# Re-fitted clock weights and a shared transfer queue in the list scheduler of a delta-rule attention and two-MoE kernel

## The chip, the cores and the metric

The kernel runs on one core of a Trainium2 chip. The metric is the device time of one execution in microseconds (us), here the median of three runs. The engines are TensorE (PE in the profile; PEld its weight loads), VectorE (DVE), ScalarE (ACT), GpSimd (POOL) and SyncE (SP), which only issues DMA transfers.

## What is computed

Three layers follow each other; the second takes the output of the first as its tokens, the third that of the second.

```python
# 1. delta rule, 4 x 8 heads, 768 positions, head size 48
k_n = k / (norm(k) + 1e-6)
for t in range(768):
    y[:, :, t] = q[:, :, t] @ state
    v_old = k_n[:, :, t] @ state
    state = state + beta[:, :, t] * outer(k_n[:, :, t], v[:, :, t] - v_old)
# 2. gated feed-forward, 3072 tokens x 384, inner size 2048
h = x @ w_in
g = h * sigmoid(h)
x = g @ w_out
# 3. eight experts, inner size 1024, every token through each of them
P = exp(x @ w_gate - max); eight rounds: rows to sum 1, columns to sum 1, P *= N / E
out = sum over e of P[:, e] * (relu(x @ w1[e]) @ w2[e])
```

## The kernel before, in words

The delta rule is worked in twelve steps of 64 positions (names end in the step: z2, c11_0; the last digit is the half of the heads). In each step the Gram products of the keys and queries (gk, gkq, gq, lines 360 to 475) give triangular systems; their inverse is worked out for two steps at a time on DVE in operations on the tiles nu and tu (line 520 on), goes to DRAM (rd, td) and comes back as rt and td11 (line 589). PE then merges it (z and r, line 609), reads the state (c, line 640), updates (d, line 657), gives the output (y) and the state's change (s, line 674) and transposes the output into tokens (t, line 707). DVE adds s to the state xs.

Two steps fill a block of 512 tokens of the second layer. For each of its 16 slices, PE makes h (x @ w_in, nine matmuls of 512 columns, line 740), ACT, DVE and POOL gate it (sg, g), and PE adds g @ w_out into x2p (line 782). Each fp32 operand is split in two parts for three products. During the first block DVE and ACT split the weights too, in seven DVE pieces per slice pair (wr, wt, lines 894 to 905). When a block is done, its logits l follow (line 831). There are six blocks; the fourth to sixth overlap the later steps. The third layer begins at about 743 us: 64 blocks of 15 products p (line 1213) and their outputs o (line 1300), with sums and residuals on DVE and POOL (line 1022) and the eight normalisation rounds beside the first of them.

No order is written out by hand. Every operation is handed to `class Order` with an engine, a cost in us, its predecessors and a priority (`op = sc.add`). `emit` walks a modelled time: at each turn it takes, of the operations that are ready first on an engine, the one of highest priority, and at the end writes all of them out by modelled start. On the chip each engine executes its own list in that order. The modelled time has four parts that matter here: `ready` adds a latency for a predecessor on another engine (LAT) and none for one on the same; `pe` models the granted clock of TensorE by slices of time, in which every PE operation leaves its weight `cols`, and a slice runs at full speed if the one before it gathered FULL; SP's transfers share one queue, in which each starts when the one before has landed; ACT's few transfers are not in that queue but have a fixed latency of 2.2 or 2.3 us. `narrow` marks the groups of small matmuls, which the model charges for a change of tiling. Before the first product of the second layer `emit` fills waits of PE with dummy matmuls (`idle`).

Of the kernel before, what the change touches and what calls it, by code (L numbers as in the profile page):

```python
# [26 lines left out]
NF = DFF // 128  # L27
# [29 lines left out]
class Order:  # L57


    QUEUES = ("SP",)  # L60
    LAT = {"PE": 0.2, "ACT": 0.16, "DVE": 0.14, "POOL": 0.1, "SP": 0.08}
# [7 lines left out]
    TICK, PHASE, FULL = 10.24 / 3, 2.63, 2000  # L69

    def add(self, engine, cost, fn, deps=(), prio=1.5, take=(), turn=None, cols=768, port=False):

        d = [x if isinstance(x, tuple) else (x, None) for x in deps]
        self.ops.append((engine, cost, fn, d, prio, take, turn, cols, port))
        return len(self.ops) - 1
# [57 lines left out]

    def emit(self, idle=None):
        self.cols, busy = {}, False
# [7 lines left out]
        while any(left.values()):  # L143
# [36 lines left out]
            else:  # L180
                if e == "PE":
                    busy = busy or cols == 4608
                    now[e] = max(now[e], IDLE)
                    while idle and not busy and t > IDLE and now[e] + 0.5 < t:
                        order.append((now[e], len(order), None))
                        now[e] = self.pe(now[e], 0.107, 256)
                    t = max(t, now[e])
                    narrow = turn == 1 and cols != 150
# [18 lines left out]
def kernel(  # L207
# [127 lines left out]
    def load_part(s, bp, part, prio):  # L335
# [4 lines left out]
        if s and not part:  # L340

            return [(op("ACT", 0.45, adma(t(a, 0), kq[s, bp, 0, :, 0]), prio=prio), 2.3),
                    (op("ACT", 0.45, adma(t(b, 0), kq[s, bp, 1, :, 0]), prio=prio), 2.3)]
# [21 lines left out]
    def gram_k(s, bp):  # L365
# [20 lines left out]
        m = op("PE", 1.07, pe, O["ke", s, bp] + ([(O["gm", s], 0.0)] if bp else []), prio=30, take=["a"] + ([] if bp else ["g"]), turn=1, cols=1088)  # L386
# [9 lines left out]
    def gram_kq(s, bp):  # L396
# [20 lines left out]
        q = op("PE", 1.07, lambda: pe(1), ld, prio=prio, take=["a"], turn=1, cols=1088)  # L417
        m = [op("PE", 1.07, lambda: pe(0), ld + [(q, 0.0)], prio=prio, take=["a"], turn=1, cols=1088), q]
# [10 lines left out]
    def units(j):  # L429
# [3 lines left out]
        for s in (2 * j, 2 * j + 1):  # L433
            for q in range(4):
# [6 lines left out]
                O["nl", j].append(op(by, 0.45 if by == "ACT" else 0.58, go, O["nd", s] + free, prio=20 if j == 0 else 3))  # L441
# [8 lines left out]
    def gram_q(s, bp):  # L450
# [13 lines left out]
        m = op("PE", 1.07, pe, O["ld", s][bp] + [O["td2", 0]], prio=5, take=["a"], turn=1, cols=1088)  # L464
# [55 lines left out]
    def tri(j, prio):  # L520
# [13 lines left out]
        if j < 2:  # L534
            roots.append(root_act(lambda: (dg, du[:, 0]), 32, [(x, 2.2 if sc.ops[x][0] == "ACT" else None) for x in O["nl", j]]
# [53 lines left out]
    def rt_load(s):  # L589
        j, o = s // 2, 64 * (s % 2)  # L590
        res = []
        for q in (1, 3, 0, 2):
# [5 lines left out]
                O["rd", j][s % 2:s % 2 + 1] + ([O["u1", s - 1, 0], O["u1", s - 1, 1]] if s else O["rt0"]), prio=12.5 + FIRST[s]))  # L598
# [7 lines left out]
        res = [(x, 2.2) if sc.ops[x][0] == "ACT" else x for x in res]  # L606
        return res, gl, t

    def merge(s):
# [19 lines left out]
        a = O["z1", s] = op("PE", 1.13, z, O["rtl", s][:2] + O["gll", s], prio=10 + FIRST[s], take=["a", "sg"], turn=1 if s else None, cols=512)  # L629
# [3 lines left out]
        c = O["r1", s] = op("PE", 1.13, r, [e1, e2] + O["tdl", s], prio=7.5 + FIRST[s], take=["a"], turn=1 if s else None, cols=512)  # L633
# [6 lines left out]
    def state_read(s, bp):  # L640
# [11 lines left out]
        a = op("PE", 1.06, pe, [O["sa", s - 1, bp]], prio=5 + FIRST[s], take=["a", "wy"], turn=1)  # L652
# [4 lines left out]
    def update(s, bp):  # L657
        x = xs[bp]

        def pe():  # L660
            w = T["w", s, bp] if s else T["kv", s][:, bp, 1]
            ps = T["d", s, bp] = psA.tile([128, H, D], F32, tag="a", name=f"d{s}_{bp}")
            for h in range(H):
                for o in (0, 64):
                    nc.tensor.matmul(out=ps[o:o + 64, h], lhsT=rt[o:o + 64, bp, h], rhs=w[o:o + 64, h], start=True, stop=True)  # L665
        a = O["u1", s, bp] = op("PE", 1.06, pe, O["rm", s] + O["rtl", s] + [O["w", s, bp] if s else O["vr", s, bp], O["xs0", bp]]
                                + ([O["h", s // 2 - 2, NF - 1]] if s >= 4 else []), prio=2 + FIRST[s], take=["a"], turn=1 if s else None)
# [783 lines left out]
```

## Time and profile before

| | |
|---|---|
| runs | 2255.64, 2266.98, 2263.58 us; median 2263.58 |
| the profiled execution | 2263.14 us, span 2261.4 us |
| mean granted clock of TensorE in it | 0.974 |
| instructions | 40411 |
| busy | PE 97%, DVE 78%, POOL 68%, ACT 45% of the span |

The span runs from the first to the last instruction; the time has 1.7 us around it. A granted clock of 1.0 is the upper of TensorE's two levels, 0.5 the lower. Times in the rows below count from the start of the span.

### The profile page before, as it was taken

The page shows a single profiled execution, that of the slowest core. Times are in us where ns is not written, and L with a number is a line of the kernel's source. Part 1 is how long each engine was busy: PE and PEld are TensorE (multiplying, and loading weights), DVE is VectorE, ACT ScalarE, POOL GpSimd, SP SyncE. Part 2 cuts the span into 40 slices and gives each one's busy share as a digit, 9 for nine tenths or more (in the row PEclk, how much of TensorE's full clock was granted, in tenths as well). Part 3 has the DMA queues.
Part 4 walks back from the last instruction along what each step waited for, and adds up shares of the span by engine and source line. Part 5 has one row for each costly group of instructions (what it writes and reads, how often), then busy time and mean ns, then how long its engine had stood idle before and what let it go on. Part 6 is the DMA issues. An engine that isn't in the chain of part 4 may idle for free.

```text
span 2261.4 us, 40411 instructions
## 1 busy us (share of the span) xinstructions
PE 2184.4 (97%) x15750; PEld 1928.4 (85%) x15750; DVE 1760.9 (78%) x2999; ACT 1023.8 (45%) x1766; POOL 1547.7 (68%) x1387
## 2 busy tenths in 40 slices
PE   8988799999999899999999999989999999999999
PEld 8877578788877778889998999979999999999998
DVE  7695857464725698888888888897888888888887
ACT  2443333334344445454444545455454444445453
POOL 0223344445337688888788888877888888888884
PEclk9887999998989899999999999999999999999999
DMA  9767132314140201101111111111101111111101
GB/s 266 186 201 167 56 72 66 81 52 95 40 108 11 84 29 31 40 29 36 35 36 36 33 38 29 43 47 39 42 29 36 36 36 36 36 36 30 42 29 50
DMA packets 127424, 136.79 MB, mean 60 GB/s; under 512 B 83392, under 2 KB 91328, under 8 KB 127232
## 3 DMA queue, kind: packets, MB, share of 16 engines
q1 hardware_dynamic: 124864, 133.55, 21.4%
q8 instruction: 124, 2.03, 0.4%
q10 hardware_dynamic: 2368, 0.66, 0.2%
q14 instruction: 68, 0.56, 0.1%
HBM read 108.47 MB, written 25.69 MB: 59 GB/s over the span
## 4 chain that ended last, share of the span: by engine, by line
PE 64%; POOL 13%; DVE 10%; DMA 5%; issue 4%; ACT 2%; SPq 1%; DVEq 0%; POOLq 0%; ACTq 0%
PE o L1300 25%; PE p L1213 20%; PE x2p L782 6%; PE h L740 5%; DVE s L1022 4%; POOL room L1022 3%; POOL wa L1022 3%; POOL wraw L1022 2%; POOL h L1022 2%; DMA ke<-in_kq 2%; PE d L665 1%; POOL wb L1022 1%; DMA nd<-ke 1%; DVE acc L1316 1%; PE y L680 1%
## 5 line engine op out<-in xcount | busy, mean ns | idle before, releaser
L1213 PE MATMUL p<-room,wa 128*128 128x512 f32 x2880 | 732.8, 395 | 2.6 <-DVE s L1022 2.6
L1213 PEld LDWEIGHTS p<-room,wa 128*128 128x128 f32 x2880 | 537.2, 189 | 95.6 <-issue 3.0
L1300 PE MATMUL o<-wb,room 128*128 128x384 f32 x2784 | 601.2, 337 | 10.6 <-POOL room L1022 3.0
L1022 DVE TENSOR_TENSOR s<-s,p 128x512 f32<-128x512 f32 x704 | 475.8, 683 | 167.8 <-ACT s L1227 85.1
L1300 PEld LDWEIGHTS o<-wb,room 128*128 128x128 f32 x2784 | 496.7, 188 | 34.8 <-DVE acc L1316 9.3
L1022 POOL TENSOR_TENSOR room<-s,room 128x512 fp32r<-128x512 f32 x232 | 321.0, 1384 | 222.0 <-ACT s L1246 117.0
L1316 DVE SCALAR_TENSOR_TENSOR acc<-o,pr,acc 128x384 f32<-128x384 f32 x708 | 415.7, 610 | 15.0 <-PE o L1300 12.6
L1300 PE MATMUL o<-wb,h 128*128 128x384 f32 x1824 | 416.5, 336 | 6.1 <-DVE acc L1316 3.7
L1300 PEld LDWEIGHTS o<-wb,h 128*128 128x128 f32 x1824 | 327.7, 188 | 27.7 <-DVE acc L1316 2.8
L1022 POOL TENSOR_TENSOR wa<-wraw,wa 128x640 fp32r<-128x640 f32 x189 | 322.4, 1718 | 2.5 <-ACT wa L1116 2.5
L1244 ACT ACTIVATE room<-s 128x512 fp32r<-128x512 f32 x232 | 145.7, 628 | 382.5 <-DVE s L1022 382.3
L1022 POOL TENSOR_TENSOR wraw<-wraw 128x256 f32<-128x256 f32 x378 | 275.0, 748 | 20.5 <-issue 10.7
L758 POOL TENSOR_TENSOR g<-sg,g 128x512 fp32r<-128x512 f32 x96 | 129.8, 1353 | 219.9 <-ACT g L754 206.0
L1246 ACT ACTIVATE s<-s 128x512 f32<-128x512 f32 x384 | 243.1, 633 | 12.2
L782 PE MATMUL x2p<-g,w 128*128 128x512 f32 x864 | 228.9, 412 | 15.5 <-DVE w L905 5.8
L1116 ACT ACTIVATE wa<-wraw 128x640 fp32r<-128x640 f32 x189 | 138.2, 731 | 224.4 <-POOL wraw L1022 213.6
L1022 DVE TENSOR_TENSOR s<-p,s 128x512 f32<-128x512 f32 x320 | 219.5, 686 | 16.7 <-PE p L1213 2.0
L740 PE MATMUL h<-x,w 128*128 128x512 f32 x864 | 216.9, 398 | 5.9 <-DVE w L905 4.1
L782 PEld LDWEIGHTS x2p<-g,w 128*128 128x128 f32 x864 | 165.1, 196 | 59.3 <-POOL g L758 10.7
L1022 POOL TENSOR_TENSOR h<-s,h 128x512 fp32r<-128x512 f32 x152 | 208.7, 1373 | 7.9 <-ACT s L1246 7.8
L1022 DVE TENSOR_TENSOR s<-s,s 128x512 f32<-128x512 f32 x192 | 207.3, 1080 | 2.5
L740 PEld LDWEIGHTS h<-x,w 128*128 128x128 f32 x864 | 161.6, 190 | 44.2 <-DVE w L905 5.9
(177 smaller groups left out, 2260.9 us busy)
## 6 DMA issues: line engine op xcount, KB each, us to landing
wraw<-in_w SPq DMA_DIRECT2D x126, 384.0 KB, 3.0
kv<-in_kv SPq DMA_DIRECT2D x12, 768.0 KB, 5.8
ke<-in_kq SPq DMA_DIRECT2D x40, 192.0 KB, 4.4
kqp<-in_kq SPq DMA_DIRECT2D x40, 192.0 KB, 4.0
nd<-ke SPq DMA_DIRECT2D x20, 256.0 KB, 4.1
gd<-ke SPq DMA_DIRECT2D x20, 256.0 KB, 2.8
kqp<-gd SPq DMA_DIRECT2D x40, 128.0 KB, 3.8
wr<-in_w_in SPq DMA_DIRECT2D x6, 768.0 KB, 5.8
```

Of the source, the lines that this page charges most:

```text
L665: nc.tensor.matmul(out=ps[o:o + 64, h], lhsT=rt[o:o + 64, bp, h], rhs=w[o:o + 64, h], start=True, stop=True)
L680: nc.tensor.matmul(out=ps[0:64, h], lhsT=t(slice(0, 112), 1)[:, h], rhs=x[0:112, 0, h], start=True, stop=True)
L740: nc.tensor.matmul(out=ps.rearrange("p (s t) -> p s t", s=2), lhsT=w[:, k, wl], rhs=X1[:, at, k, xl], start=n == 0, stop=n == 8)
L758: nc.gpsimd.tensor_tensor(out=g[:, 1], in0=T["sg", b, f], in1=f32(g)[:, 0], op=ALU.subtract)
L782: nc.tensor.matmul(out=T["x2p", b][j], lhsT=w[:, wl, 128 * j:128 * j + 128], rhs=g[:, gl], start=f == 0 and n == 0, stop=f == NF - 1 and n ...
L1022: e.tensor_tensor(out=out, in0=in0, in1=in1, op=o)
L1116: nc.scalar.activation(P2[key][:, :, 0], R(3 + 5 * g, 8 + 5 * g), AF.Copy)
L1213: nc.tensor.matmul(out=ps, lhsT=w[:, i, wl], rhs=x[:, xl], start=k == 0, stop=k == 2)
L1244: nc.scalar.activation(P2[key][:, 0], buf(x), AF.Relu)
L1246: op2("ACT", 0.52, lambda: nc.scalar.activation(buf(x), buf(x), AF.Relu), writes=[("s", n, x)], prio=PR_H)
L1300: nc.tensor.matmul(out=ps, lhsT=h[:, hl, 128 * i:128 * i + 128], rhs=w[:, wl], start=c == 0, stop=c == 5)
L1316: op2("DVE", 0.53, lambda A=A, pk=pk, t=t: nc.vector.scalar_tensor_tensor(out=A(), in0=P2[pk], scalar=P2["pr"][:, t, e:e + 1], in1=A(), op ...
```

## The change

The planner's model changes, and no operation does. A predecessor on the same engine now costs a small latency (OWN). A slice of time now also gets KEEP for having been fast itself (`fast`), FULL is halved and PHASE shifted, and the weights `cols` are other numbers for each kind of matmul: an h or x2p product, the reference with 4608 before and 1430 now, against a Gram product 1088 and 520, z and r 512 and 221, c 768 and 240, d 768 and 390, y 1440 and 480, s 768 and 530, t 768 and 241, logits 150 and 0, the third layer's products 1536 and 477, its outputs 2304 and 716, a dummy 256 and 80. `narrow` is told by these numbers. ACT's transfers (`lands`) now pass through the queue model of SP's. Line numbers move by 10 or so.

```diff
+    OWN = {"PE": 0.0, "DVE": 0.12, "ACT": 0.12, "POOL": 0.11, "SP": 0.08}
...
-    TICK, PHASE, FULL = 10.24 / 3, 2.63, 2000
+    TICK, PHASE, FULL, KEEP = 10.24 / 3, 2.53, 1000, 120
...
-                lat = 0.0 if own == engine and engine not in self.QUEUES else self.LAT[own]
+                lat = self.LAT["SP"] if self.ops[d][9] else (self.OWN if own == engine else self.LAT)[own]
...
-            k = int((t - self.PHASE) / self.TICK + 1 + 1e-6)
-            c = cost if self.cols.get(k - 1, 0) >= self.FULL else 1.85 * cost
+            k = max(0, int((t - self.PHASE) / self.TICK + 1 + 1e-6))
+            c = cost if self.fast(k) else 1.85 * cost
...
+    def fast(self, k):
+        if k < 1:
+            return False
+        if k not in self.full:
+            self.full[k] = self.cols.get(k - 1, 0) + self.KEEP * self.fast(k - 1) >= self.FULL
+        return self.full[k]
...
-                    narrow = turn == 1 and cols != 150
+                    narrow = cols in (520, 221, 240, 390, 480, 530)
...
+                    if self.ops[i][9]:
+                        end[i] = queue = max(t + 1.5, queue) + self.ops[i][9]
                     if self.ops[i][8]:
-                        port[e] = end[i]
+                        port[e] = now[e]
...
-            return [(op("ACT", 0.45, adma(t(a, 0), kq[s, bp, 0, :, 0]), prio=prio), 2.3),
+            return [op("ACT", 0.45, adma(t(a, 0), kq[s, bp, 0, :, 0]), prio=prio, lands=0.42),
...
-        m = op("PE", 1.07, pe, O["ke", s, bp] + ([(O["gm", s], 0.0)] if bp else []), prio=30, take=["a"] + ([] if bp else ["g"]), turn=1, cols=1088)
+        m = op("PE", 1.07, pe, O["ke", s, bp] + ([(O["gm", s], 0.0)] if bp else []), prio=30, take=["a"] + ([] if bp else ["g"]), turn=1, cols=520)
...
-                              prio=2, take=["m"], turn=0, cols=4608)
+                              prio=2, take=["m"], turn=0, cols=1430)
```

What it moves, by the order of instructions on each engine, stands here at three places.

PE, from the h product of slice seven of the first block to the merge z2 of step two. Before:

```order
L740 MATMUL h0_7_2288<-x1_106,w12_2174 128x512 x9
L405 MATMUL gkq9_1_1_2326<-ke9_1_2304 64x64
L405 MATMUL gkq9_1_0_2348<-ke9_1_2304 64x64
L405 MATMUL gkq10_0_1_2373<-ke10_0_2312 64x64
L782 MATMUL x2p0_0_1804<-g0_6_2322,w12_2174 128x512 x3
L782 MATMUL x2p0_0_1804<-g0_7_2365,w12_2174 128x512 x3
L405 MATMUL gkq10_0_0_2430<-ke10_0_2312 64x64
L614 MATMUL z2_2453<-rt_93,td11_94 32x32 x32
```

Now:

```order
L750 MATMUL h0_7_2217<-x1_106,w12_2121 128x512 x9
L415 MATMUL gkq8_1_0_2240<-ke8_1_2101 64x64
L792 MATMUL x2p0_0_1781<-g0_6_2238,w12_2121 128x512 x3
L624 MATMUL z2_2298<-rt_93,td11_94 32x32 x32
L792 MATMUL x2p0_0_1781<-g0_7_2269,w12_2121 128x512 x3
```

Each Gram row stands for a group of 16 matmuls, each x2p row for the first three of nine. The Gram products of the keys of steps nine and ten left the place and come later; z2 has one group of each kind ahead of it, where it had six groups.

DVE, around the state updates (xs) of steps two and three; wt and wr are tiles of a weight that is split. Before:

```order
L750 TENSOR_TENSOR sg0_9_2595<-h0_9_2555,sg0_9_2595 128x512
L701 TENSOR_TENSOR xs0_91<-xs0_91,s2_0_2662 48x384 x2
L701 TENSOR_TENSOR xs1_92<-xs1_92,s2_1_2811 48x384 x2
L701 TENSOR_TENSOR xs0_91<-xs0_91,s3_0_2941 48x384 x2
L894 TENSOR_SCALAR wt20_2343<-wt20_2343 128x768
L895 TENSOR_SCALAR wt20_2343<-wt20_2343 128x768
L897 SCALAR_TENSOR_TENSOR wt20_2343<-wr5_2141,wt20_2343 128x768
L750 TENSOR_TENSOR sg0_10_3141<-h0_10_3112,sg0_10_3141 128x512
```

Now:

```order
L760 TENSOR_TENSOR sg0_9_2477<-h0_9_2445,sg0_9_2477 128x512
L711 TENSOR_TENSOR xs0_91<-xs0_91,s2_0_2482 48x384 x2
L711 TENSOR_TENSOR xs1_92<-xs1_92,s2_1_2619 48x384 x2
L904 TENSOR_SCALAR wt20_2273<-wt20_2273 128x768
L905 TENSOR_SCALAR wt20_2273<-wt20_2273 128x768
L907 SCALAR_TENSOR_TENSOR wt20_2273<-wr5_2088,wt20_2273 128x768
L711 TENSOR_TENSOR xs0_91<-xs0_91,s3_0_2848 48x384 x2
L711 TENSOR_TENSOR xs1_92<-xs1_92,s3_1_2891 48x384 x2
L913 TENSOR_SCALAR wr5_2088<-wt20_2273 128x768
L760 TENSOR_TENSOR sg0_10_3031<-h0_10_3004,sg0_10_3031 128x512
```

Rows in between are left out. The first five pieces of weight 20 went from behind step three's first state update to ahead of it.

PE, from the state read c11_1 of the last step to the first h product of the last block. Before, with no 512-column product from y10_0 on:

```order
L647 MATMUL c11_1_7640<-xs1_92,kqp1_86 64x48
L831 MATMUL l8_7659<-wgr_64,x2_8_0_7458 128x16
L665 MATMUL d11_0_7674<-wq11_0_7638,rt_93 64x48 x16
L665 MATMUL d11_1_7703<-wq11_1_7672,rt_93 64x48 x16
L681 MATMUL y11_0_7726<-xs0_91,kqp0_85 64x48
L681 MATMUL y11_1_7749<-xs1_92,kqp1_86 64x48
L713 MATMUL t11_0_7768<-ident_62,y11_0_7766 128x128 x3
L831 MATMUL l9_7774<-wgr_64,x2_9_0_7691 128x16
L713 MATMUL t11_1_7789<-ident_62,y11_1_7772 128x128 x3
L740 MATMUL h5_0_7819<-x1_106,w0_227 128x512 x9
```

Now:

```order
L750 MATMUL h4_15_7551<-x1_106,w29_3383 128x512 x9
L723 MATMUL t10_1_7563<-ident_62,y10_1_7561 128x128 x3
L657 MATMUL c11_1_7613<-xs1_92,kqp1_86 64x48
L792 MATMUL x2p4_0_6900<-g4_15_7606,w31_3513 128x512 x3
L675 MATMUL d11_0_7641<-wq11_0_7611,rt_93 64x48 x16
L691 MATMUL y11_0_7690<-xs0_91,kqp0_85 64x48
L723 MATMUL t11_0_7732<-ident_62,y11_0_7730 128x128 x3
L841 MATMUL l8_7738<-wgr_64,x2_8_0_7658 128x16
L723 MATMUL t11_1_7753<-ident_62,y11_1_7736 128x128 x3
L841 MATMUL l9_7773<-wgr_64,x2_9_0_7757 128x16
L750 MATMUL h5_0_7812<-x1_106,w0_236 128x512 x9
```

The last products of block four, h4_15 and x2p from g4_13 to g4_15, moved in among the small groups of steps ten and eleven, and the logits l8 moved behind t11_0.

## Rows read from the trace of the kernel before

**Rows 1.** The page's busy times, all engines.

```profile
PE 2184.4 (97%) x15750; PEld 1928.4 (85%) x15750; DVE 1760.9 (78%) x2999; ACT 1023.8 (45%) x1766; POOL 1547.7 (68%) x1387
```

**Rows 2.** Busy time by stage; stretch, us, PE PEld DVE ACT POOL busy, clock, DMA, GB/s.

```profile
0.00:262.50 262.50, 229.08 (x3650) 199.13 (x3650) 196.54 (x471) 104.86 (x178) 65.73 (x69) 0.88 0.69 183
262.50:743.40 480.90, 462.58 (x4572) 378.70 (x4571) 262.77 (x487) 177.96 (x322) 235.16 (x223) 0.96 0.27 65
743.40:2261.40 1518.00, 1492.73 (x7532) 1350.59 (x7530) 1301.59 (x2043) 741.02 (x1266) 1246.76 (x1096) 1.00 0.12 38
```

**Rows 3.** The same view, five stretches of the first two stages.

```profile
460.22:467.01 6.79, 6.79 (x199) 6.18 (x198) 4.93 (x11) 2.34 (x5) 1.87 (x3) 1.00 0.57 153
548.56:571.42 22.86, 22.52 (x450) 21.05 (x450) 12.13 (x27) 7.23 (x17) 11.13 (x14) 0.70 0.49 141
644.47:669.32 24.85, 21.74 (x486) 20.37 (x485) 8.43 (x19) 9.88 (x22) 3.98 (x6) 0.79 0.24 65
182.50:212.50 30.00, 28.19 (x642) 25.71 (x638) 14.48 (x26) 11.22 (x22) 19.97 (x21) 0.77 0.77 172
212.50:274.00 61.50, 46.44 (x334) 34.54 (x334) 55.97 (x122) 21.02 (x38) 14.15 (x12) 0.92 0.25 73
```

**Rows 4.** Chain of waits, 640 to 680 us: start us, us, what.

```profile
652.35 1.13 issue
...
654.51 1.00 issue
...
659.30 3.58 PE d L665 x64
...
667.11 0.11 PE l L832
...
668.33 0.42 PE t L713 x3
```

**Rows 5.** Chain of waits, 150 to 225 us.

```profile
174.92 1.13 PE z L614 x64
...
181.71 2.00 PE d L665 x64
```

**Rows 6.** Timeline of PE from 667 us: start us, us, what, [idle before <-releaser].

```profile
669.32 8.38 PE L740 MATMUL h<-x,w 128*128 128x512 f32 x27 [0.58 <-ACT x L716]
```

**Rows 7.** Chain of waits, 610 to 640 us.

```profile
611.47 2.04 PE h L740 x9
...
628.68 0.14 issue
```

**Rows 8.** Timeline of POOL in one block of the second MoE.

```profile
991.09 1.30 POOL L1022 TENSOR_TENSOR room<-s,room 128x512 fp32r<-128x512 f32 x1
992.34 1.02 POOL L1022 TENSOR_TENSOR wb<-wraw,wb 128x384 fp32r<-128x384 f32 x1
```

**Rows 9.** Timeline of PE in the same block.

```profile
995.36 0.68 PE L1300 MATMUL o<-wb,h 128*128 128x384 f32 x3
```

**Rows 10.** Timeline of SP at the start.

```profile
14.63 1.92 SPq L439 DMA_DIRECT2D nu<-nd  x4
16.65 0.43 SPq L385 DMA_DIRECT2D nd<-gneg  x1
```

**Rows 11.** Timeline of DVE at the start.

```profile
24.04 0.19 DVE L479 TENSOR_SCALAR rta<-nu 128x32 f32<-128x32 f32 x1 [3.55 <-DMA nu<-nd]
```

**Rows 12.** Timeline of DVE, 180 to 222 us.

```profile
187.94 1.12 DVE L701 TENSOR_TENSOR xs<-xs,s 48x384 f32<-48x384 f32 x2 [4.78 <-PE s L697]
...
212.57 1.09 DVE L894 TENSOR_SCALAR wt<-wt 128x768 f32<-128x768 f32 x1
...
215.77 0.95 DVE L901 SCALAR_TENSOR_TENSOR wr<-wr 128x768 int32<-128x768 int32 x1
```

**Rows 13.** Timeline of PE from 155 us.

```profile
154.92 4.38 PE L740 MATMUL h<-x,w 128*128 128x512 f32 x18
```

**Rows 14.** Timeline of SP ahead of the first rt loads.

```profile
167.05 4.46 SPq L595 DMA_DIRECT2D rt<-rd  x4
```

More of the change, by code (lines that the diff above doesn't have):

```diff
@@ L67, in __init__, with add @@
         self.pools, self.slot = {k: [()] * n for k, n in pools.items()}, {}
-    TICK, PHASE, FULL = 10.24 / 3, 2.63, 2000
-    def add(self, engine, cost, fn, deps=(), prio=1.5, take=(), turn=None, cols=768, port=False):
+    TICK, PHASE, FULL, KEEP = 10.24 / 3, 2.53, 1000, 120
+    def add(self, engine, cost, fn, deps=(), prio=1.5, take=(), turn=None, cols=0, port=False, lands=None):
         d = [x if isinstance(x, tuple) else (x, None) for x in deps]
-        self.ops.append((engine, cost, fn, d, prio, take, turn, cols, port))
+        self.ops.append((engine, cost, fn, d, prio, take, turn, cols, port, lands))
         return len(self.ops) - 1
@@ L132, in pe @@
         return t
+    def fast(self, k):
[4 more added lines that the diff above has]
+        return self.full[k]
     def emit(self, idle=None):
-        self.cols, busy = {}, False
+        self.cols, self.full, busy = {}, {}, False
         left, wait, then = {}, [len(o[3]) for o in self.ops], {}
@@ L181, in emit @@
                 if e == "PE":
-                    busy = busy or cols == 4608
+                    busy = busy or cols == 1430
                     now[e] = max(now[e], IDLE)
@@ L340, in load_part @@
         if s and not part:
-            return [(op("ACT", 0.45, adma(t(a, 0), kq[s, bp, 0, :, 0]), prio=prio), 2.3),
-                    (op("ACT", 0.45, adma(t(b, 0), kq[s, bp, 1, :, 0]), prio=prio), 2.3)]
+            return [op("ACT", 0.45, adma(t(a, 0), kq[s, bp, 0, :, 0]), prio=prio, lands=0.42),
+                    op("ACT", 0.45, adma(t(b, 0), kq[s, bp, 1, :, 0]), prio=prio, lands=0.42)]
         return [op("SP", 0.42, dma(t(a, part), kq[s, bp, 0, :, part]), after, prio=prio),
@@ L440, in go @@
                         out=nu[r0:r0 + 16], in_=T["nd", s][32 * q:32 * q + 32, :, c0:c0 + 32].rearrange("r u c -> u r c"))
-                O["nl", j].append(op(by, 0.45 if by == "ACT" else 0.58, go, O["nd", s] + free, prio=20 if j == 0 else 3))
+                O["nl", j].append(op(by, 0.45 if by == "ACT" else 0.58, go, O["nd", s] + free, prio=20 if j == 0 else 3,
+                                    lands=0.58 if by == "ACT" else None))
     def mask_q(s, bp):
@@ L534, in tri @@
         if j < 2:
-            roots.append(root_act(lambda: (dg, du[:, 0]), 32, [(x, 2.2 if sc.ops[x][0] == "ACT" else None) for x in O["nl", j]]
+            roots.append(root_act(lambda: (dg, du[:, 0]), 32, list(O["nl", j])
                                   + ([O["td2", j - 1]] if j else []), 8, -1.0))
@@ L597, in rt_load @@
                 in_=T["rd", j][r0:r0 + 16].rearrange("u (c r) -> c u r", r=32)),
-                O["rd", j][s % 2:s % 2 + 1] + ([O["u1", s - 1, 0], O["u1", s - 1, 1]] if s else O["rt0"]), prio=12.5 + FIRST[s]))
+                O["rd", j][s % 2:s % 2 + 1] + ([O["u1", s - 1, 0], O["u1", s - 1, 1]] if s else O["rt0"]), prio=12.5 + FIRST[s], lands=0.58 if by == "ACT" else None))
         free = [O["z1", s - 1], O["r1", s - 1]] if s else []
@@ L632, in merge @@
         sc.free(a, "a", [e1, e2])
-        c = O["r1", s] = op("PE", 1.13, r, [e1, e2] + O["tdl", s], prio=7.5 + FIRST[s], take=["a"], turn=1 if s else None, cols=512)
+        c = O["r1", s] = op("PE", 1.13, r, [e1, e2] + O["tdl", s], prio=7.5 + FIRST[s], take=["a"], turn=1 if s else None, cols=221)
         sc.free(a, "sg", [c])
@@ L785, in moe_o @@
         a = O["o", b, f] = op("PE", 2.045, pe, O["g", b, f] + O["wout", f] + prev, prio=4.5,
-                              take=["x"] if f == 0 else [], turn=0, cols=4608)
+                              take=["x"] if f == 0 else [], turn=0, cols=1430)
         sc.free(O["g", b, f][0], "g", [a])
@@ L836, in cp @@
             nc.scalar.activation(T["l2", b], T["l", b][:, :, 1], AF.Copy)
-        m = op("PE", 1.25, logit, ev + [O["wg"]], prio=2, take=["a"], turn=1, cols=150)
+        m = op("PE", 1.25, logit, ev + [O["wg"]], prio=2, take=["a"], turn=1)
         e = op("ACT", 0.12, cp, [m] + ([O["lg", b - 1]] if b else []), prio=-3.5)
@@ L1274, in products @@
             O["p", n, r] = P2["pe"] = op2("PE", 0.694, pe(r), reads=[("x", r), ("wa", wn(n), OPERAND[r][0])], writes=[("p", n, r)],
-                               deps=first + [(P2["pe"], 0.0)], take=[k], turn=2, cols=1536, prio=PR_P)
+                               deps=first + [(P2["pe"], 0.0)], take=[k], turn=2, cols=477, prio=PR_P)
             if r in then:
@@ L1339, in go @@
                 fn(P2["sk", n])
-            return op2("PE", cost, go, reads=["pr"], writes=[("sk", n)], deps=[(lastw["pr"], 1.5)], take=["m"], prio=PR_S, cols=64)
+            return op2("PE", cost, go, reads=["pr"], writes=[("sk", n)], deps=[(lastw["pr"], 1.5)], take=["m"], prio=PR_S)
         def dve(cost, fns, n=None):
```

23 lines of the change are left out of this document (11 added, 12 removed).

## The prediction

> **What bounds the kernel now.** I read the page's busy times, then the busy time by stage, then the stretches of the first two stages in which the granted clock is low, and in those the chain of waits and the timelines of PE, DVE and SP.
>
> PE is busy for 97% of the span [rows 1]. By stage [rows 2]: the second MoE, 743.40 to 2261.40, has PE busy for 1492.73 of 1518.00 us at a granted clock of 1.00, so an order can give back 25 us there at the very most. The first two stages hold 743.4 us, and there the clock is 0.88 and 0.96. A clock of 0.5 is the lower level (1.2 GHz), 1.0 the upper (2.4 GHz); 0.88 over 262.5 us means (1 - 0.88) x 262.5 = 31 us in which PE got nothing for its time, idle stretches among them, and 0.96 over 480.9 means 19 us. That is the stock from which this change, which only sorts the same operations, can draw.
>
> The change moves the clock's weights, so the question is where the clock falls. The stretches [rows 3] show it: during steps nine (548.56 to 571.42) and ten/eleven (644.47 to 669.32) the clock is 0.70 and 0.79. In the first of them PE is busy for 22.52 of 22.86 us; the reader is to see that it falls there although PE has hardly a gap, in a run of small matmuls with no 512-column product of the first MoE among them. A shorter run of the same kind, step seven (460.22 to 467.01, 6.79 us), stays at 1.00. What the low level costs one group: an update d takes 3.58 us for both halves [rows 4] where it takes 2.00 at the upper level [rows 5]; and the first three h products after the run, 27 matmuls, take 8.38 us [rows 6] where nine take 2.04 [rows 7], so 8.38 - 6.12 = 2.26 us too much.
>
> **The change, part by part.** Nothing is removed and no operation is new; the count of idle dummy matmuls at the start changes by nine. All terms are moves.
>
> *Second MoE: 0.* PE's order is the same but for the small Sinkhorn matmuls. On POOL, in nearly each of 64 blocks one wb piece (1.02 us) goes ahead of the two relu residuals issued before it, h and room. In one block room ends at 991.09 + 1.30 = 992.39 [rows 8], and the outputs that read these two start at 995.36 [rows 9]; with the piece of 992.34 ahead it would end at 993.41, 1.95 us early still. The residual that feeds the block's later outputs keeps its place. Were the cover gone, it would cost up to 1 us a block; I take 0, with +1 us in all as the bound.
>
> *Steps ten and eleven: -6 (-3 to -9).* Now: 24.85 us [rows 3], of which (1 - 0.79) x 24.85 = 5.2 us are lost to the clock, 1.13 + 1.00 = 2.1 are waits of c11 for the state [rows 4], 0.58 is the wait of h5_0 [rows 6]; add 2.26 for the h products behind. That is 10.2 us over the work. In the new order the triangular inverse of these steps is issued about three iterations earlier (an h and a w_out product each, 4.1 us), z10 stands behind h4_11, and the w_out products of g4_13, g4_14 and g4_15 and the product h4_15 stand among the small ones, which took 2.04 us each. What runs bare is only from d11_0 to l9: two updates (2.00 [rows 5]), two outputs y (priced like half an update each, 1.0), two transposes (0.42) and two logits (668.33 - 667.11 = 1.2 each [rows 4]): 7.2 us, near the 6.79 us that kept the clock [rows 3]. If the clock holds, the 5.2 and the 2.26 come back, 7.5 of the 10.2. Against that l9 now follows l8 by one transpose and may wait a microsecond or so for its operand. I take 6. Lower end: the bare stretch runs at the clock that the long one had, which loses 7.2 x 0.21 / 0.79 = 1.9, the 2.26 stay, c11's waits stay, 0.58 stays: 7 left, gain 3. Upper end: all but 1.1 of c11's waits: 9.
>
> *Step nine: -1 (0 to -6).* One wide product, that of g3_15, moves from ahead of s8_1 to between t8_1 and s8_1. The bare stretch shrinks from 22.86 x 0.70 = 16.0 us of work to some 14.7; at the same clock the loss goes from 6.9 to 6.3. Were the product enough to hold the clock, 6 would come back.
>
> *The first stage: -5 (+4 to -13).* Two things carry it. At the start, the second nd1 put was issued at 16.65, behind four nu loads of 1.92 us in all [rows 10]; the last nu loads need it, and DVE stood still for 3.55 us until 24.04 [rows 11]. The put now stands before the nu loads: it can go 2.0 us earlier, they 0.4 later. I take -1.5 (0 to -2). Then DVE: from 182.5 to 212.5 it has 14.48 us of work in 30, while from 212.5 to 274.0 it has 55.97 in 61.5 and PE only 46.44 [rows 3], since the products wait for weights that DVE splits. The first weight of that second stretch begins at 212.57, behind the state update of step three; its first five pieces run from there to 215.77 + 0.95 = 216.72, 4.1 us with two short steps of the inverse among them [rows 12], and now stand ahead of that update, in the slack stretch, where the one wait shown is 4.78 us [rows 12]. If all of this goes into idle time, the saturated stretch ends 4.1 us sooner; I take -3.5. Bounds: the same 4.1 us stand in front of the state update and the chain of steps is late by it (+4.1); or the fuller PE also keeps the clock in 182.5 to 212.5, (1 - 0.77) x 30 = 6.9 more (-11). The other moves of this stage (Gram products pushed behind step three, key loads with them) fill or leave gaps that PE has either way; the rival D is about them.
>
> *Latencies on the same engine and ACT's transfers in the shared queue* change no wait on the chip by themselves: 0.
>
> The sum: 2263.1 (the profiled execution; the median of the three runs shown is 2263.58) - 5 - 1 - 6 - 0 = **2251 us**. The ends together: 2263.1 - 13 - 6 - 9 = 2235 and 2263.1 + 4 - 3 + 0 + 1 = 2265, rounded up to 2266.
>
> A measurement of this kernel tells some 0.5%, 11.3 us, from no change: faster is under 2252, slower over 2275.
>
> **The rule that speaks against the main term.** In steps ten and eleven the two waits of c11 stand just ahead of the stretch in which d took 3.58 [rows 4], so these rows alone would also fit a clock that falls for the gaps. Against it stands step nine, with 0.34 us of idle time and a clock of 0.70. The Trainium skill, TensorE: Matmul & The Clock Gate, section "HAM oscillation — how this bites in real kernels", puts a falling clock down to idle gaps of PE between bursts. By that rule the small products themselves would keep the clock and the change would gain little at the end, a sum of about 2257; step nine's row disagrees with it as the only cause.
>
> **The rivals.**
> - A, chance 0.15: the clock falls for the gaps. c11 still comes right behind s10_1 and DVE's addition of the state, so its waits (2.1 us) stay, and with them the slow d and h behind. Of the late term only about 0 to 1 is left: 2263.1 - 5 - 1 = **2257**. For it: the place of the waits. Against it: step nine.
> - B, chance 0.15: the first stage gives nothing. DVE executes in order, and one of its multiplies (sg of h0_3) and the moved weight pieces wait for POOL's roots or for wr loads; what the slack stretch takes in, the state update loses. 2263.1 - 1 - 6 = **2256**. For it: the longest DVE wait shown there, 4.78 us, ends with PE's s [rows 12]: it is a place behind a dependency, not free time at large. Against it: PE still waits for weights behind it.
> - C, chance 0.10: the change doesn't do what it says. The new weights describe the clock no better, the wide products that now stand at the end are missing elsewhere, and the low level moves with them: **2263**.
> - D, chance 0.10, slower: a z stands ahead of its data. Between the end of h0_7 (154.92 + 4.38 = 159.30) [rows 13] and z2 at 174.92 [rows 5] PE now does six groups; in the new order only one Gram group (about 1.1) and one product (2.05) are left there. The four rt loads that z2 reads were issued from 167.05 on, 4.46 us in all [rows 14]. If they come no sooner, PE stands 174.92 - 162.45 = 12.4 us in front of z2 with all products behind it. The same at z10, which goes ahead by two products and their h, 8.2 us; it starts now 0.14 us after its rt [rows 7]. 2263.1 + 12.4 + 8.2 - 6 - 1 = **2277**. It decides from the point at which rt lands no earlier than now; against it: between the last put of step nine's keys and rt SP now issues two pairs of key loads and two weight loads, of which one pair of keys stays, and the inverse for z10 moved further than z10 did.
>
> **How the numbers follow.** The forecast, both gains, has 0.50. Its own range is 2235 to 2260, and with about 0.8 of it under 2252 that gives 0.40 faster; A gives 0.03 of its 0.15 there, B 0.04: 0.47. The rest of these, and C, are within 0.5%: 0.43. D is the 0.10 slower. The range 2235 to 2266 holds the forecast, A, B and C; it leaves out D and the tails.
>
> **What would show it.** Right: in the new profile the stretch from y10_0 to h5_0 shows a clock over 0.9 and the first three h products of the last block take near 6.1 us; DVE's saturated stretch ends 3 to 4 us sooner; the second MoE still takes 1518 us within 1. Wrong: c11's waits stand with a slow d11 behind (A); the time from 0 to z4 is unchanged (B); the low-clock stretches are as long as before, elsewhere (C); PE idle for over 5 us in front of z2 or z10 (D). A second MoE that differs by more than 3 us would show that my 0 for POOL was wrong.

## The result: 1.2% slower, all of it in the second MoE

The changed kernel takes 2287.81 us (median of 4 runs, 2284.39 to 2293.97) against 2261.99 us of the kernel before (median of 4 runs, 2255.64 to 2266.98): a ratio of 1.0119, 95% interval 1.0083 to 1.0154. That is outside the range of the prediction, on the side that was given 0.10. The profiled execution took 2284.39 us with a span of 2282.6 us and a mean granted clock of 0.98. Of the runs of all kernels below, one of pool_more (4204.75 us) was far slower than the rest and is left out of its ratio.

The page's busy times of the changed kernel, for [rows 1]:

```profile
PE 2185.0 (96%) x15747; PEld 1906.0 (83%) x15747; DVE 1784.5 (78%) x2999; ACT 1027.5 (45%) x1766; POOL 1546.2 (68%) x1387
```

DVE is busy 23.6 us longer. PE's busy time is the same to 0.6 us, but only in the sum of two opposite changes: by the stages below it is 14.2 us less in the first two layers and 14.9 us more in the second MoE. The busy time by stage, cut where [rows 2] is cut (the first h of the second block, the first product of the second MoE), with the same columns:

```profile
0.00:256.80 256.80, 221.60 (x3646) 190.76 (x3646) 196.05 (x474) 104.93 (x177) 63.18 (x69) 0.90 0.74 191
256.80:731.30 474.50, 455.83 (x4574) 372.20 (x4571) 259.17 (x484) 178.38 (x323) 239.52 (x223) 0.97 0.27 64
731.30:2282.60 1551.30, 1507.60 (x7532) 1343.01 (x7531) 1329.25 (x2043) 744.19 (x1266) 1243.51 (x1096) 0.99 0.12 37
```

The reader is to see two opposite results in one. The second MoE begins at 731.3 where it began at 743.4, which is the 12 us that the prediction hoped for, though half of it is the luck of these two traces (the means over the traces of either order of the first two layers lie 5.9 us apart, see the part on the prediction); and it lasts 1551.3 us where it lasted 1518.0, a change that the prediction had put at 0 (at most +1). In it DVE is busy 27.7 us longer (1329.25 against 1301.59) for the same 2043 instructions. The clock is not the reason: in the second MoE it stood at its lower level for 16.2 us before and 17.1 us now. Which instructions of DVE, the costliest groups show, with the group of POOL's residuals (room) below them. Before:

```profile
L1022 DVE TENSOR_TENSOR s<-s,p 128x512 f32<-128x512 f32 x704 | 475.8, 683 | 167.8 <-ACT s L1227 85.1
...
L1022 DVE TENSOR_TENSOR s<-s,s 128x512 f32<-128x512 f32 x192 | 207.3, 1080 | 2.5
...
L1022 POOL TENSOR_TENSOR room<-s,room 128x512 fp32r<-128x512 f32 x232 | 321.0, 1384 | 222.0 <-ACT s L1246 117.0
```

Now:

```profile
L1032 DVE TENSOR_TENSOR s<-s,p 128x512 f32<-128x512 f32 x704 | 476.0, 684 | 189.0 <-ACT s L1237 152.9
...
L1032 DVE TENSOR_TENSOR s<-s,s 128x512 f32<-128x512 f32 x192 | 253.2, 1319 | 2.4
```

The additions with one operand in PSUM (s<-s,p) take the same time within a nanosecond. Those with both operands in SBUF (s<-s,s, three in each of the 64 blocks) went from 1080 to 1319 ns, 46 us in all (DVE's busy time grew by less, since the records of neighbouring instructions overlap). And PE's wait for DVE's accumulation, in the second MoE 5.9 us in 10 places before, is now, in the list of waits of that stage (us in total, times, the longest):

```profile
PE o L1310 <- DVE acc L1326: 22.1, 55, 1.2
```

Why an addition grows is in the timelines of one steady block. Before, DVE's three s<-s,s and what POOL did meanwhile:

```profile
1956.38 0.69 DVE L1022 TENSOR_TENSOR s<-s,s 128x512 f32<-128x512 f32 x1
...
1959.43 0.87 DVE L1022 TENSOR_TENSOR s<-s,s 128x512 f32<-128x512 f32 x1
...
1962.14 1.40 DVE L1022 TENSOR_TENSOR s<-s,s 128x512 f32<-128x512 f32 x1
```

```profile
1951.95 4.49 POOL L1022 TENSOR_TENSOR wraw<-wraw 128x256 f32<-128x256 f32 x6
1956.40 1.82 POOL L1022 TENSOR_TENSOR room<-s,room 128x512 fp32r<-128x512 f32 x1
1958.18 3.55 POOL L1022 TENSOR_TENSOR wa<-wraw,wa 128x640 fp32r<-128x640 f32 x2
1961.70 1.29 POOL L1022 TENSOR_TENSOR h<-s,h 128x512 fp32r<-128x512 f32 x1
```

The same place in the changed kernel:

```profile
1946.10 1.57 DVE L1032 TENSOR_TENSOR s<-s,s 128x512 f32<-128x512 f32 x1
...
1950.03 1.84 DVE L1032 TENSOR_TENSOR s<-s,s 128x512 f32<-128x512 f32 x1
...
1953.70 0.68 DVE L1032 TENSOR_TENSOR s<-s,s 128x512 f32<-128x512 f32 x1
```

```profile
1941.68 3.80 POOL L1032 TENSOR_TENSOR wraw<-wraw 128x256 f32<-128x256 f32 x5
1945.83 1.29 POOL L1032 TENSOR_TENSOR room<-s,room 128x512 fp32r<-128x512 f32 x1 [0.35 <-PE p L1223]
1947.07 1.19 POOL L1032 TENSOR_TENSOR wraw<-wraw 128x256 f32<-128x256 f32 x1
1948.23 3.09 POOL L1032 TENSOR_TENSOR wa<-wraw,wa 128x640 fp32r<-128x640 f32 x2
```

One swap on POOL is the difference between these rows: its six weight sums (wraw) ran through before, now the last of them stands behind the first residual room of the block (of the sum c1). Of an s<-s,s and one of these POOL instructions, the one that starts second waits for the first. Before, the sums kept POOL until DVE had begun: DVE's addition took 0.69, and room took 1.82 instead of 1.29. Now room begins at 1945.83, as soon as what it waits for is there, and DVE's addition, 0.27 us later, ends at 1947.67, that is 0.55 us after room's end at 1947.12. The second one ends at 1951.87, 0.55 us after the two wa pieces (1948.23 + 3.09 = 1951.32). The third one before (1962.14 + 1.40 = 1963.54) ends 0.55 after h (1961.70 + 1.29 = 1962.99). The Trainium skill, SBUF — State Buffer, section "Who interferes with whom", says just this: a DVE instruction with two SBUF inputs contends with a GpSimd instruction that reads SBUF, and the order of issue decides which one blocks until the other has ended. The trace agrees in each of these additions. (In 15 of the 192 additions before, POOL's next instruction began within some hundredths of a microsecond of the addition; there the addition ended 0.55 us after that one.)

At the end of it PE waits for the accumulation behind the first addition. Six products some 11 us earlier with the outputs behind them, and the six ahead of this wait:

```profile
1936.56 1.55 PE L1223 MATMUL p<-room,wa 128*128 128x512 f32 x6
1937.95 0.69 PE L1310 MATMUL o<-wb,h 128*128 128x384 f32 x3
...
1947.69 1.55 PE L1223 MATMUL p<-room,wa 128*128 128x512 f32 x6
1949.64 0.79 PE L1310 MATMUL o<-wb,room 128*128 128x384 f32 x3 [0.40 <-DVE acc L1326]
1950.28 0.68 PE L1310 MATMUL o<-wb,h 128*128 128x384 f32 x3
```

From the start of the six to the start of the output it is 1.39 us without the wait and 1.95 with it, 0.56 more; only 0.40 of that shows as idle time, since PE's matmuls overlap in the trace. The three outputs then take 0.64 to the next start instead of 0.52. Together that is 0.68 us, most of what a block loses.

A block (from its first product to the next block's; median of blocks 4 to 62) took 22.98 us before and 23.75 now. It took over 23.4 us in 12 of 63 blocks before and in 55 now. Blocks 0 to 9 lose nothing in sum (244.2 and 243.6 us) and some later ones were slow before as well, so the stage loses 33.3 us and not 64 x 0.77 = 49.

### The profile page after: what moved, and what is told of

It is laid out like the page before. It is cut to its first block, busy times and chain, and to the rows that moved or that the text cites. A ratio compares the mean times of both kernels' runs of the same rounds, so it can differ in the third digit from the quotient of the medians.

```text
span 2282.6 us, 40405 instructions
## 1 busy us (share of the span) xinstructions
PE 2185.0 (96%) x15747; PEld 1906.0 (83%) x15747; DVE 1784.5 (78%) x2999; ACT 1027.5 (45%) x1766; POOL 1546.2 (68%) x1387
## 4 chain that ended last, share of the span: by engine, by line
PE 50%; POOL 22%; DVE 13%; issue 7%; DMA 5%; ACT 2%; SPq 1%; POOLq 0%; DVEq 0%; ACTq 0%
PE o L1310 17%; PE p L1223 14%; DVE s L1032 7%; PE x2p L792 6%; POOL wa L1032 6%; PE h L750 6%; POOL room L1032 4%; POOL h L1032 4%; POOL wraw L1032 3%; POOL wb L1032 2%; DVE acc L1326 2%; DMA ke<-in_kq 1%; PE d L675 1%; ACT wa L1126 1%; POOL du L542 1%
## 5 line engine op out<-in xcount | busy, mean ns | idle before, releaser
L1310 PE MATMUL o<-wb,room 128*128 128x384 f32 x2784 | 610.6, 341 | 25.7 <-DVE acc L1326 20.4
L1223 PEld LDWEIGHTS p<-room,wa 128*128 128x128 f32 x2880 | 537.3, 189 | 100.5 <-issue 6.5
L1310 PEld LDWEIGHTS o<-wb,room 128*128 128x128 f32 x2784 | 487.4, 188 | 74.2 <-DVE acc L1326 54.3
L1032 POOL TENSOR_TENSOR room<-s,room 128x512 fp32r<-128x512 f32 x232 | 307.2, 1329 | 265.1 <-ACT s L1256 247.6
L1032 POOL TENSOR_TENSOR wraw<-wraw 128x256 f32<-128x256 f32 x378 | 302.2, 814 | 13.0 <-PE h L750 3.2
L1032 POOL TENSOR_TENSOR wa<-wraw,wa 128x640 fp32r<-128x640 f32 x189 | 297.5, 1587 | 0.6 <-ACT wa L1126 0.6
L1032 DVE TENSOR_TENSOR s<-s,s 128x512 f32<-128x512 f32 x192 | 253.2, 1319 | 2.4
L1256 ACT ACTIVATE s<-s 128x512 f32<-128x512 f32 x384 | 243.6, 634 | 12.2
L792 PE MATMUL x2p<-g,w 128*128 128x512 f32 x864 | 227.9, 410 | 16.2 <-POOL g L768 6.9
L1032 POOL TENSOR_TENSOR h<-s,h 128x512 fp32r<-128x512 f32 x152 | 218.6, 1438 | 8.1 <-ACT s L1256 6.8
```

The lines of the kernel that those rows point to most:

```text
L792: nc.tensor.matmul(out=T["x2p", b][j], lhsT=w[:, wl, 128 * j:128 * j + 128], rhs=g[:, gl], start=f == 0 and n == 0, stop=f == NF - 1 and n ...
L1032: e.tensor_tensor(out=out, in0=in0, in1=in1, op=o)
L1223: nc.tensor.matmul(out=ps, lhsT=w[:, i, wl], rhs=x[:, xl], start=k == 0, stop=k == 2)
L1256: op2("ACT", 0.52, lambda: nc.scalar.activation(buf(x), buf(x), AF.Relu), writes=[("s", n, x)], prio=PR_H)
L1310: nc.tensor.matmul(out=ps, lhsT=h[:, hl, 128 * i:128 * i + 128], rhs=w[:, wl], start=c == 0, stop=c == 5)
```

## The experiments

Four parts of the change can be planned apart: the clock weights, ACT's transfers in the queue, and OWN in the first two layers or in the second MoE. The orders they give show that OWN alone moves the second MoE. **Theory 1**: the 33 us are that order. **Rival 2**: they come from the state in which the second MoE now starts. Within theory 1, **1a** is the POOL swap, **1b** the other moves.

**OWN in the first two layers alone (own_first).** In the changed kernel:

```diff
-                lat = self.LAT["SP"] if self.ops[d][9] else (self.OWN if own == engine else self.LAT)[own]
+                lat = self.LAT["SP"] if self.ops[d][9] else ((self.OWN2 if i >= self.second else self.OWN) if own == engine else self.LAT)[own]
```

Here `second` is the first operation of the second MoE and OWN2 is 0 for all engines but SP.

> The changed kernel, but the latency between operations of the same engine (OWN) holds in the first two layers only; in the second MoE it is 0 again, as before the change. The order of the first two layers is then that of the changed kernel in all but a few places, and the order of the second MoE that of the kernel before. Theory 1 (the loss is the order of the second MoE, and OWN alone moved it): the second MoE takes 1518 us again, within 3, and the whole 1518 + 731 + 2 = 2251 us, faster than both kernels. Rival 2 (the second MoE is slow because it begins 12 us earlier and out of another state, whatever its order): it takes some 1551 us as in the changed kernel, the whole 2284 us.

Measured: 2248.83 us, 0.9960 of the kernel before (0.9944 to 0.9976); in the trace the second MoE took 2255.4 - 737.8 = 1517.6 us, a block 22.98. (The three groups of runs that follow were made on different chips; each ratio is against the kernel before on the same one, whose medians were 2258.45, 2259.22 and 2260.40 us.)

**OWN in the second MoE alone (own_second).** The same line in the kernel before, with OWN 0 and OWN2 as the change has it.

> The kernel before, with OWN added for the operations of the second MoE alone; the first two layers keep their order. Theory 1: the second MoE takes 1551 us within 5, the whole 743 + 1551 + 2 = 2296 us. Rival 2: 1518 us and 2263 us, since the start of the second MoE is that of the kernel before.

Measured: 2290.92 us, 1.0139 (1.0113 to 1.0166); 2293.9 - 740.4 = 1553.5 us from the start at 740.4, a block 23.74. Rival 2 falls with both: the start at 740.4 did not save this kernel, that at 737.8 did not spoil the other. The trace of clock_only below is closer still to the changed kernel's start: from 733.2 us its second MoE, in the old order, took 1516.9.

**One engine's OWN at a time (own_pool, own_dve, no_pool).** OWN2 for POOL alone, for DVE alone, for DVE and ACT. For POOL alone the steady block differs from that before by the one swap.

> The changed kernel, with OWN in the second MoE for POOL alone. In a steady block one pair of instructions stands the other way round than in the kernel before: the last of POOL's six weight sums goes behind the residual of c1. Theory 1a (that swap puts POOL's sum and the two wide weight pieces beside DVE's additions s<-s,s, and these grow): s<-s,s near 1.3 us instead of 1.08, about 23.75 us a block, 2280 to 2285 us. Rival 1b (the swap is harmless; what costs is that POOL's wb piece and ACT's copies stand elsewhere): 22.98 us a block, 2251 us.

> The changed kernel, with OWN in the second MoE for DVE alone. In a steady block POOL's first wb piece then stands ahead of two residuals, ACT's two wb copies stand apart and DVE takes one addition behind an output; the six weight sums stand as before the change. Theory 1a: 22.98 us a block, s<-s,s near 1.08 us, 2251 us in all. Rival 1b: 23.75 us a block, 2280 to 2285 us.

> The changed kernel, with OWN in the second MoE for DVE and ACT but not for POOL: all moves of the change in a steady block but the one of POOL's last weight sum (wb ahead of two residuals, ACT's evacuation of the first product behind two more copies, one DVE addition an output later). If that one swap is the whole loss: 22.98 us a block and 2249 us. If the other moves take part: between 2260 and 2288 us.

Measured: own_pool 2298.47 us, 1.0178 (1.0155 to 1.0201); own_dve 2248.66, 0.9962 (0.9946 to 0.9977); no_pool 2252.86, 0.9960 (0.9947 to 0.9974). A block: 23.89, 22.98, 22.98. The row of s<-s,s on the page, of own_pool and of own_dve:

```profile
L1035 DVE TENSOR_TENSOR s<-s,s 128x512 f32<-128x512 f32 x192 | 256.3, 1335 | 2.5
```

```profile
L1035 DVE TENSOR_TENSOR s<-s,s 128x512 f32<-128x512 f32 x192 | 204.4, 1065 | 2.4
```

So 1a holds in kind and 1b falls: one swapped pair of POOL instructions in each block makes the loss. It does so against either background: in a steady block own_pool differs from the kernel before, and the changed kernel from no_pool, by this pair alone on DVE, ACT and POOL, and a block goes from 22.98 to 23.89 and to 23.75. The size was not foreseen: by itself the swap costs 44 us (the second MoE of own_pool takes 1561.7 in its trace), 10 us more than with the other moves beside it; why they give that back was not tried. The wb pieces, of which alone the prediction spoke, cost nothing.

**More work on POOL (pool_more).** In own_pool:

```diff
-            (3, lambda: tt("POOL", R(13, 16), R(2, 5), bc(R(5, 6), 3), SUB)),
+            (3, lambda: [tt("POOL", R(13, 16), R(2, 5), bc(R(5, 6), 3), SUB) for _ in range(2)]),
```

> The slow kernel own_pool with more work: POOL's fifth weight sum is made twice in each block (1.03 us more on POOL), everything else in the same order. Theory 1a in its sharp form (of POOL's residual of c1 and DVE's addition s<-s,s, the one that starts second waits for the first to end; in the slow order the residual starts 0.3 us ahead): the repeated sum keeps POOL busy until after DVE has started, the first s<-s,s of a block goes from 1.57 to 0.7 us, a block takes 22.98 us and the whole some 2250 us although POOL has more to do. Rival 1c (the slow order makes POOL late with what PE and ACT need): a block takes 24 us or more, the whole 2298 us or more.

Measured: 2297.48 us, 1.0162 (1.0125 to 1.0199), a block 23.79: not the 22.98 of 1a's sharp form. The additions and POOL in one block:

```profile
1954.18 1.02 DVE L1035 TENSOR_TENSOR s<-s,s 128x512 f32<-128x512 f32 x1
...
1957.56 1.57 DVE L1035 TENSOR_TENSOR s<-s,s 128x512 f32<-128x512 f32 x1
...
1960.96 1.40 DVE L1035 TENSOR_TENSOR s<-s,s 128x512 f32<-128x512 f32 x1
```

```profile
1952.52 2.12 POOL L1035 TENSOR_TENSOR wraw<-wraw 128x384 f32<-128x384 f32 x2
1954.60 1.75 POOL L1035 TENSOR_TENSOR room<-s,room 128x512 fp32r<-128x512 f32 x1
...
1957.00 3.55 POOL L1035 TENSOR_TENSOR wa<-wraw,wa 128x640 fp32r<-128x640 f32 x2
1960.52 1.28 POOL L1035 TENSOR_TENSOR h<-s,h 128x512 fp32r<-128x512 f32 x1
```

The first addition did get ahead of room, which now takes 1.75, but it waited for the repeated sum (1952.52 + 2.12 = 1954.64, and 0.56 more is its end). And POOL, later by the repeated work, then met the third addition, which had been free in own_pool: 1.40 instead of 0.68. PE's wait for acc moved to a later place in the block. That an s<-s,s waits for the POOL instruction before it holds in each row; that the first of the three decides alone does not.

Rival 1c has the number of the whole nearly right (2298 us), but not what PE waits for. In 13 steady blocks these are all of PE's waits that the traces of the changed kernel, of own_pool and of pool_more list (us in total, times, the longest); that of the kernel before lists none:

```profile
PE o L1310 <- DVE acc L1326: 5.1, 13, 0.4
...
PE o L1313 <- DVE acc L1329: 3.9, 13, 0.3
...
PE o L1313 <- DVE acc L1329: 3.5, 13, 0.3
```

It is DVE's accumulation once in each block, and never POOL.

**Less work on POOL (first_less).** In own_first:

```diff
-            (2, lambda: tt("POOL", R(16, 18), P2["R"][:, 3:6:2], bc(R(0, 1), 2), SUB)),
+            (2, lambda: n or tt("POOL", R(16, 18), P2["R"][:, 3:6:2], bc(R(0, 1), 2), SUB)),
```

> The quick kernel own_first with less work: POOL's sixth weight sum is made in the first block alone and its old value used after that (0.75 us less on POOL per block), everything else in the same order. This leaves out part of the weights of the second MoE. Theory 1a in its sharp form: POOL is free when the residual of c1 becomes ready, starts it some 0.3 us ahead of DVE's addition, the first s<-s,s of a block goes from 0.69 to 1.5 us or so, and a block takes 23.7 us: 2280 to 2298 us although POOL has less to do. Rival 1c: 22.98 us a block, 2249 us.

Measured: 2260.15 us, 0.9993 (0.9975 to 1.0010). That is slower than own_first, by 7.5 us by the ratios and 11 us by the medians (on two chips), with 0.75 us less for POOL to do in each block. The first addition went from 0.69 to 1.57 us (medians of blocks 36 to 62), as expected, and a block to 23.19: the sign was right, the size (0.21 us a block) under a third of the 0.72 that was expected. The third addition came free at the same time (1.40 to 0.68).

**Shorter POOL instructions (pool_split).** In own_pool:

```diff
-                tt("POOL", P2[key][:, :, 1], R(3 + 5 * g, 8 + 5 * g), f32(P2[key])[:, :, 0], SUB)
+                for a, b in ((0, 2), (2, 3), (3, 5)):
+                    tt("POOL", P2[key][:, a:b, 1], R(3 + 5 * g + a, 3 + 5 * g + b), f32(P2[key])[:, a:b, 0], SUB)
```

> The slow kernel own_pool, in which POOL's wide weight pieces wa (640 columns, 1.54 us each when alone) are made in three instructions of 256, 128 and 256 columns: the same work and order, about 0.4 us more on POOL for each piece, 1.2 us a block. Theory 1d (a DVE addition s<-s,s that starts during a POOL instruction waits for that instruction's end, and a block is longer by what the three additions of a block wait beyond some 3.1 us in sum): the second addition of a block, 1.84 us beside wa, goes to 1.3 us or less, the sum of the three from 4.1 to about 3.5 us, a block from 23.89 to 23.2 or 23.4 us, the whole from 2298 to 2260 to 2272 us, although POOL has more to do. Rival 1c (POOL is late with its work): 2298 us or more.

Measured: 2297.90 us, 1.0157 (1.0132 to 1.0181), a block 23.85. The second addition went from 1.84 to 0.68, further than expected, but the third from 0.68 to 1.69, and nothing was gained: theory 1d's times for the block and the whole were missed. The whole is where rival 1c had it, but here too the only wait of PE in the steady blocks is the one for DVE's accumulation (5.5 us in 13 blocks).

The medians over blocks 36 to 62, with the sum of the three additions beside the length of a block:

| kernel | first | second | third | sum | block |
|---|---|---|---|---|---|
| before | 0.69 | 0.88 | 1.39 | 2.96 | 22.98 |
| own_dve | 0.69 | 0.89 | 1.39 | 2.97 | 22.98 |
| no_pool | 1.54 | 1.15 | 0.69 | 3.38 | 22.98 |
| first_less | 1.57 | 1.15 | 0.68 | 3.40 | 23.19 |
| pool_split | 1.57 | 0.68 | 1.69 | 3.94 | 23.85 |
| pool_more | 1.02 | 1.58 | 1.40 | 4.00 | 23.79 |
| own_pool | 1.56 | 1.84 | 0.68 | 4.08 | 23.89 |
| changed | 1.57 | 1.84 | 0.68 | 4.09 | 23.75 |

The length of a block goes with the sum rather than with any one of the three: the four kernels with a sum of 3.4 us or less take 22.98 to 23.19, the four with about 4 take 23.75 to 23.89. That is a description and not a shown law: at 3.38 and 3.40 the blocks lie 0.21 us apart, and among the four slow ones the larger sum does not have the longer block. No experiment took a wait away without another coming in its place, so what one wait alone costs is not shown either. Why the waits in the slow orders fall so that the sum stays near 4, whichever of them is relieved, is open.

**What gives the gain of the first two layers (clock_only, own1_only, clock_lands).** The clock weights alone; OWN in the first two layers alone; the clock weights and the queue.

> The kernel before with only the new clock weights (cols, FULL, KEEP, PHASE, narrow); no OWN, and ACT's transfers with the fixed latency of before. The second MoE is then in the order of before. Theory C (the gain of the first two layers comes from the clock weights): the second MoE starts near 736 us and the whole is 2249 us like own_first. Rival O (it comes from OWN in the first two layers): 2258 to 2260 us, start near 742.

> The kernel before with only OWN, and that in the first two layers alone. Theory C: no gain, 2258 us, the second MoE starts near 742 us. Rival O: start near 736 us, 2249 to 2252 us.

> The changed kernel without OWN anywhere: the new clock weights and ACT's transfers in the shared queue. The second MoE is in the order of before. Theory C (clock weights and the queue carry the gain of the first two layers): second MoE from about 736 us, 2249 to 2252 us. Rival O (OWN carries part of it): 2254 us or more.

Measured: clock_only 2255.67 us, 0.9983 (0.9965 to 1.0001); own1_only 2255.35, 0.9978 (0.9962 to 0.9994); clock_lands 2259.53, 0.9992 (0.9973 to 1.0010). By the runs theory C is not borne out: neither the clock weights nor these with the queue give a gain that can be told from none. Rival O's 2249 to 2252 us was missed too; OWN alone gives 0.2%. In the traces the second MoE began at 733.2, 738.5 and 736.0 us, which looks like C, but the traced executions of clock_only and clock_lands were among the quickest of their twelve (2251.82 and 2253.05 us). All three parts together, with the second MoE as before or nearly so, give 0.4% (own_first, own_dve, no_pool). Their intervals overlap that of OWN alone, so it is open how the 0.4% divides; a lucky order among several is as good an account as any part's merit.

**The version that beats both** is own_first (or own_dve): the change without OWN in the second MoE (or with it for DVE alone), 2249 us against 2258.45 of the kernel before beside it.

## Why the prediction was wrong, point by point

**The step that failed** is "*Second MoE: 0*": "I take 0, with +1 us in all as the bound". It measured +33.3 us, and the prediction's own sign against it, a second MoE that differs by more than 3 us, came true. The step looked at one of POOL's moves, wb ahead of two residuals, and asked only whether the readers of the moved piece would still find it in time. That was right for this move (own_dve, no_pool). It left out the other move in the same lists, the sixth weight sum behind the residual of c1, which was to be seen in the order; and it never asked what stands beside a POOL instruction on DVE. The trace before had the sign of it: room took 1.30 in [rows 8] and 1384 ns in the mean on the page, and s<-s,s took 1080 ns beside 683 for the like additions with a PSUM operand. Such a duration that is not the same each time was the hint that the two engines share something, so that a move on one has a price on the other. The sentence "Were the cover gone, it would cost up to 1 us a block" is near the measured 0.77 by luck, for it priced another event (outputs that wait for their residuals), and the range did not take it in. That an order can give back 25 us of the stage at most was not contradicted (the shortest was own_dve's, 1510.5 us); what it could take away was not bounded.

**Steps ten and eleven, -6:** the size about right, the reason only in part. The stretch from the first h of block four to that of block five took 97.9 and 100.5 us in the two traces with the old order of these layers (before, own_second), and 89.6 to 93.1 in the eight with the new one: -7.6 between the means. The changed kernel's own rows for [rows 3] and [rows 6], the stretch from y10_0 to h5_0 and the 6 us behind it:

```profile
626.20:654.40 28.20, 27.39 (x526) 23.46 (x525) 9.79 (x20) 12.02 (x27) 6.25 (x9) 1.00 0.19 49
654.40:660.60 6.20, 5.96 (x20) 4.43 (x19) 0.45 (x2) 1.41 (x3) 2.81 (x5) 0.72 0.91 268
```

The clock stays at 1.00 through the stretch, which now holds four wide products as well (4 x 2.04 us), and still falls right behind it, at the first h of the last block. In own_first, with the same order of PE there, the last 14.4 us of the stretch (647.2 to 661.6) had a clock of 0.82 and the whole was only 2 us longer. From the first h of block four to that of block five PE's idle time went from 4.8 and 5.0 us to 0.8 in each of the eight: 4.1 of the 7.6 us are idle time that is gone, where the prediction had put most of its gain on the clock. And its term for the first 27 matmuls of h behind the stretch, 2.26 us, did not come back: they were to take near 6.1 us, took 8.38 and 8.24 in the old order, and 8.7 to 10.1 in the new one, slow in clock or waiting. Rival A, a clock that falls for the gaps, is not decided by this.

**Given back behind it, +3:** not foreseen. From the first h of the last block to the first product of the second MoE it took 74.1 and 73.9 us before, 76.2 to 79.5 in the eight. The waits point at POOL, weakly: in the last block PE's x2p waits for g on POOL for 3.0 us before, 5.0 in own_first and 3.8 in the changed kernel, and in the changed kernel five weight sums (658.31 to 662.06) stand ahead of the block's first g. This was not tried by itself; the cause is open.

**The first stage, -5:** mostly not there. The first h of the second block starts at 262.5 and 259.3 in the old order, at 255.8 to 262.2 in the new one, 1.4 us apart in the mean, less than the scatter of either. Both moves happened: at the start DVE goes on at 22.50 instead of 24.04, the 1.5 us of the prediction, and from 182.5 to 212.5 it has 22.49 us of work instead of 14.48, with PE's clock at 0.94 instead of 0.77. But its waits did not vanish, and where the rest of the gain went is not shown. PE's waits from 100 to 280 us, before:

```profile
PE gkq L405 <- DMA ke<-in_kq: 9.0, 4, 4.4
PE x2p L782 <- DVE w L905: 5.8, 3, 3.1
PE h L740 <- DVE w L905: 4.1, 3, 1.7
```

Now:

```profile
PE h L750 <- DVE w L915: 6.8, 4, 2.1
PE x2p L792 <- DVE w L915: 6.3, 4, 1.8
PE gkq L415 <- DMA ke<-in_kq: 3.1, 2, 2.8
...
PE z L624 <- DMA rt<-rd: 1.1, 1, 1.1
```

The waits for keys went from 9.0 to 3.1, and those for weights from 9.9 to 13.1. That is rival B in kind. The last row is rival D: z2 stands ahead of its data, but by 1.1 us and not by 12.4, since rt came earlier with it.

**Step nine, -1:** 0. From the first h of the second block to that of block four both orders take 307.8 us in the mean (306.4 to 309.9).

**The sum** of what the first two layers gave: -1.4, 0, -7.6, +3.2, in all -5.8 in the traces, where the prediction had -12; the runs of own_first, own_dve and no_pool say -7.5 to -9.8. The slower side that the prediction named, D, was the wrong mechanism; the side itself came from the term that had been set to nothing.

## What to carry to other kernels

Where a change moves an instruction of POOL or DVE, look whether one of DVE with both operands in SBUF then runs at the same time as one of POOL, and price the longer of the two, not the reader's slack alone; a group whose mean lies well above that of a like one (1080 against 683 ns) is the hint. A move that repeats in every block is priced per block, and its bound is multiplied by the count before it is called small. And a change to the model of one thing (a latency of 0.11 us that was 0) can lose more, through a move that it makes in the steady part (33 us here), than the rest of the change gains (6 to 10 us): hold the steady part of a schedule fixed when the model is refitted.

## What the runs showed of the hardware

An s<-s,s of DVE takes 0.68 to 0.69 us alone and ends 0.55 to 0.56 us after the POOL instruction that had started before it; a residual of POOL, 1.29 us alone, takes up to 1.82 when DVE was first. The additions with one PSUM operand don't notice POOL at all: all 704 of s<-s,p in that stage took 0.63 to 0.69 us, before and now. Taking 0.75 us of work from POOL in each block made the kernel 7 to 11 us slower than own_first, and adding 1.03 us made own_pool no slower (2297.48 against 2298.47 us).
